# One clamp of the weights' decode goes from VectorE to GpSimd, ahead of VectorE's steps on the low word and the sign

## The chip, the cores and the metric

The kernel runs on one core of a Trainium2 chip. The metric is the device time of one execution in microseconds. Three runs of the kernel before took 1301.26, 1301.65 and 1302.59 us; the median is 1301.65. Engines are named as in the profile: PE is TensorE (PEld its weight loads), DVE VectorE, ACT ScalarE, POOL GpSimd, SP the queue that issues most DMAs.

## The reference

Talking-heads attention (4 batches, 12 heads, 448 positions, 64 per head) feeds two feed-forward layers over 1792 tokens of 768 values:

```
scores = einsum('bhij,hg->bgij', q @ k.T / 8, w_pre);  attn = softmax(scores)
x = (einsum('bhij,hg->bgij', attn, w_post) @ v) as (1792, 768)
a = x @ w1;  b = x @ w2;  h = (a * b) @ w3;  x = h @ w_out          # 768 -> 1024 -> 1024 -> 768
h = x @ w_in;  out = max(h, 0)**2 @ w_out2                          # 768 -> 2048 -> 768
```

All weights arrive as 64-bit floats.

## The kernel before

The chip's engines have no 64-bit floats, so every weight is decoded: from the low word, the high word and the sign bit a 32-bit float is put together by bit operations. The high word's magnitude, clamped, shifted left, gives most of the bits; three bits come from the low word, and the sign from the high word again.

Everything is multiplied with split operands: a float is a high half plus a low half, and a product is three matmuls (high x high, high x low, low x high).

The program has four stages on TensorE. Up to about 500 us it runs attention, then, to 676 us, the products with w1 and w2. From 676 to 749 us stands what the title calls the weights' product: M = w3 x w_out, 1024 x 768, made once on the chip so that the tokens are multiplied with M alone (line 1198, `m_tile`). From 749 us on come the tokens' products with M (line 964, `product`), and then the last layer.

The weights' product is the stage of the change. w3 comes in 16 pieces of 128 x 512, called W1 to W16 here, in the order of `M_ORDER`; each is decoded by `decode_alone`. Its steps are: ACT takes the magnitude of the high word (line 676); DVE takes the three bits of the low word (the shift, 677) and adds the sign (680), into tile `xa`; DVE clamps the magnitude (684), shifts it (687) in tile `zt`, and joins both by an exclusive or (690). Then `one_steps` copies the weight to a high half on ACT (872), and POOL subtracts to get the low half (875). There are 16 copies of these, three buffers for `xa`, one for `zt`, two for the raw weight.

TensorE spends 24 matmuls on each of W1 to W12: four rows of w_out, six matmuls each, over two halves `o` of M's 768 columns. The first two of a row's three kinds of matmul want the high half of the weight, the third its low half. W13 to W16 are used twice, 12 matmuls each time: first for half 0 of the columns, then for half 1. When two pieces of M are ready, `keep_m` copies them from PSUM (ACT, 1181) and DVE takes their largest magnitudes (982, tile `mx`).

When a half of M is complete, `scale_m` finds one scale for it: the largest value is turned by TensorE (1227), reduced on DVE (1230), spread over the partitions by TensorE (1236), and DVE makes the scale (109 to 114, 1242). Then `halves_steps` splits the 8 tiles of that half: high halves on ACT (1129), low halves on DVE (1125). The tokens' products that follow are called c0, c1, c2 (they need half 0 of M) and c3 to c5 (half 1), 24 matmuls each; each is copied from PSUM by ACT (1327), and then DVE reduces it (982, tile `xm`). The next layer's weights are decoded meanwhile (703 to 717).

The order on each engine is written out when the program is built. A stream of steps for the weights (`weight_steps`) stands beside the products; each step names an engine and an assumed cost. `tick` moves an assumed clock on after every few matmuls, and each stream then issues its steps as long as the assumed load of their engine (`busy`) is not too far ahead of that clock; a step marked REST waits for a time on it, and `after(E)` until engine E's assumed load is done. POOL steps cost nothing there. So a changed list of costs or rests changes what stands between what on an engine.

Of the kernel before, what the change touches and what calls it, by code (L numbers as in the profile page):

```python
# [14 lines left out]
ALU = mybir.AluOpType  # L15
# [5 lines left out]
F64_LEAST = 2.0 ** -15 * 1.125  # L21
F64_MOST = float.fromhex("0x1.dffffep+16")
# [13 lines left out]
def talking_heads_attention_moe_moe2(  # L36
# [15 lines left out]
    nc = tc.nc  # L52
# [612 lines left out]
    def after(eng):  # L665
        return REST, Behind(eng), None

    def decode_alone(raw, n):

        lo, hi = (raw.rearrange("p (f two) -> p f two", two=2)[:, :, w] for w in (0, 1))  # L670
        x = pools["w"].tile([P, DM], F32, tag="xa", name="xa", bufs=3)[:, :n]
        zt = pools["w"].tile([P, DM], F32, tag="zt", name="zt", bufs=1)[:, :n]
        xi, zi = x.bitcast(I32), zt.bitcast(I32)
        r = n / DM
        return x, [
            (ACT, 0.9 * r, lambda: nc.scalar.activation(zt, hi.bitcast(F32), AF.Abs)),
            (DVE, 0.55 * r, lambda: nc.vector.tensor_scalar(
                xi, lo, 29, 0x40000000, op0=ALU.logical_shift_right, op1=ALU.bitwise_or
            )),
            (DVE, 0.95 * r, lambda: nc.vector.scalar_tensor_tensor(  # L680
                xi, hi, -(2 ** 31), xi, op0=ALU.bitwise_and, op1=ALU.bitwise_or
            )),
            after(ACT),
            (DVE, 0.55 * r, lambda: nc.vector.tensor_scalar(
                zt, zt, F64_LEAST, F64_MOST, op0=ALU.max, op1=ALU.min
            )),
            (DVE, 0.55 * r, lambda: nc.vector.tensor_scalar(
                zi, zi, 4, 1, op0=ALU.logical_shift_left, op1=ALU.logical_shift_right
            )),
            (DVE, 0.95 * r, lambda: nc.vector.tensor_tensor(xi, zi, xi, op=ALU.bitwise_xor)),  # L690
            after(DVE),
        ]

# [29 lines left out]
    ACT, DVE, POOL, REST, GATE = range(5)  # L723
# [794 lines left out]
```

## Time and profile before

| | us |
|---|---|
| median of three runs | 1301.65 |
| the profiled execution | 1300.97 |
| its span, first to last instruction | 1299.2 |
| PE busy | 1264.7 (97%) |
| DVE busy | 981.1 (76%) |
| ACT busy | 697.0 (54%) |
| POOL busy | 444.5 (34%) |

The granted clock of TensorE is 0.997 of full speed over the span, and 1.00 in the stage of the change. A busy TensorE over the span does not mean that it is busy everywhere: the time of a stage is read from that stage's rows. A duration in the timeline begins when the instruction begins on its engine, and it holds what the instruction itself waited for in hardware; what stands in brackets behind a row is the idle time of the engine just before it, and who ended it.

### The profile page before, as it was taken

What the parts mean: (1) busy time and instruction counts of PE and PEld (TensorE: products, weight loads), DVE (VectorE), ACT (ScalarE), POOL (GpSimd) and SP (SyncE); (2) the same over time, 40 slices, a digit from 0 to 9 for tenths busy, and PEclk for the clock granted to TensorE, in tenths of its full rate; (3) what the DMA queues carried; (4) which work ended last, traced back from release to release, by engine and by line L of the source; (5) the groups of instructions that cost most, each with busy time, mean ns of one, the idle gap of its engine ahead of it and who ended that gap; (6) DMA issues with size and microseconds to landing.
All of it is one profiled execution on the core that took longest, in us unless ns stands there. A gap on an engine that the chain in (4) does not pass through costs nothing.

```text
span 1299.2 us, 25896 instructions
## 1 busy us (share of the span) xinstructions
PE 1264.7 (97%) x10173; PEld 778.9 (60%) x10173; DVE 981.1 (76%) x2036; ACT 697.0 (54%) x1349; POOL 444.5 (34%) x511
## 2 busy tenths in 40 slices
PE   7999999999999899999999999999999999999998
PEld 3676766666766655555569855555555555555555
DVE  5888798788888858877649677336659788797776
ACT  3877876887886535544324354236853453534420
POOL 3899789889877701100002201000000100001000
PEclk9999999999999899999999999999999999999999
DMA  6466555645647624434414332303131322224004
GB/s 176 116 161 158 132 145 135 156 127 149 162 113 196 193 78 94 114 101 99 145 47 138 109 78 56 31 5 86 37 78 45 104 58 60 78 37 109 10 9 170
DMA packets 82174, 132.92 MB, mean 102 GB/s; under 512 B 30820, under 2 KB 67812, under 8 KB 82052
## 3 DMA queue, kind: packets, MB, share of 16 engines
q1 hardware_dynamic: 75636, 121.87, 35.0%
q0 software_dynamic: 2992, 5.42, 2.9%
q10 hardware_dynamic: 3424, 3.98, 1.1%
q8 instruction: 80, 1.31, 0.5%
q14 instruction: 42, 0.34, 0.1%
HBM read 80.78 MB, written 11.92 MB: 71 GB/s over the span
## 4 chain that ended last, share of the span: by engine, by line
PE 86%; DVE 5%; DMA 2%; issue 2%; POOL 2%; ACT 2%; SPq 0%; POOLq 0%; ACTq 0%; DVEq 0%
PE mm L964 40%; PE mm L1395 17%; PE p L272 9%; PE o L365 7%; PE s L232 5%; PE a L476 4%; PE mm L1198 3%; DMA Bt<-S 2%; DVE ATl L387 1%; DVE EL L352 1%; PE p L964 1%; DVE st L286 1%; POOL EH L338 1%; ACT ATh L381 1%; DVE Vl L455 1%
## 5 line engine op out<-in xcount | busy, mean ns | idle before, releaser
L964 PE MATMUL mm<-x,w 128*128 128x448 f16 x2196 | 416.7, 352 | 0.9 <-DVE th L999 0.9
L964 PEld LDWEIGHTS <-w 128*128 128x128 f16 x2304 | 225.0, 98 | 210.4 <-issue 1.3
L1395 PE MATMUL mm<-w,g 128*128 128x384 f16 x1344 | 219.7, 326 | 0.0
L1395 PEld LDWEIGHTS <-g 128*128 128x128 f16 x1344 | 131.5, 98 | 87.4 <-issue 0.2
L272 PE MATMUL p<-Bt,wpre_k 120*120 120x448 f32 x360 | 162.6, 570 | 7.8 <-DMA Bt<-S 3.9
L338 POOL TENSOR_SCALAR EH<-E,st 120x448 f16<-120x448 f32 x180 | 135.7, 764 | 61.6 <-DVE st L324 46.5
L365 PEld LDWEIGHTS <-EH 120*112 120x112 f16 (+1 forms) x1440 | 126.1, 131 | 50.2 <-issue 40.1
L387 DVE TENSOR_TENSOR ATl<-o,ATh 112x480 f16<-112x480 f32 x180 | 116.2, 646 | 39.5 <-ACT ATh L381 39.4
L381 ACT CAST ATh<-o 112x480 f16<-112x480 f32 x180 | 101.1, 562 | 65.2 <-PE o L365 57.5
L365 PE MATMUL o<-wph,EH 120*112 120x120 f16 x720 | 125.7, 220 | 6.1 <-DVE ATl L387 4.5
L294 ACT ACTIVATE E<-p,st 120x448 f32<-120x448 f32 x180 | 116.1, 645 | 22.7 <-DVE st L286 10.2
L729 POOL DMA_DIRECT2D across<-tot x23 | 12.8, 557 | 323.9 <-ACT xa L715 323.9
L365 PE MATMUL o<-wph,EL 120*112 120x120 f16 x720 | 123.5, 217 | 0.0
L365 PE MATMUL o<-wpl,EH 120*112 120x120 f16 x720 | 123.5, 217 | 0.0
L1404 DVE SCALAR_TENSOR_TENSOR acc<-mm,sv,acc 128x384 f32<-128x384 f32 x196 | 112.1, 611 | 14.2 <-PE mm L1395 13.5
L286 DVE TENSOR_REDUCE st<-p 120x1 f32<-120x448 f32 x180 | 110.2, 612 | 7.8 <-PE p L272 7.5
L964 PE MATMUL mm<-h,M 128*128 128x448 f16 x576 | 109.4, 352 | 0.0
L350 POOL TENSOR_TENSOR EL<-F,EH 120x448 f16<-120x448 f32 (+1 forms) x90 | 101.1, 1123 | 7.5
L243 ACT COPY S<-s 110x896 f32<-110x896 f32 (+1 forms) x92 | 84.0, 913 | 27.7 <-PE s L232 27.4
L715 ACT ACTIVATE xa<-xa 128x768 f32<-128x768 f32 x56 | 47.1, 842 | 91.7 <-DVE xa L711 76.3
L365 PEld LDWEIGHTS <-EL 120*112 120x112 f16 x720 | 94.3, 131 | 0.0
L352 DVE SCALAR_TENSOR_TENSOR EL<-E,st,EH 120x448 f16<-120x448 f32 (+1 forms) x90 | 82.5, 917 | 13.3 <-POOL EH L338 12.9
(194 smaller groups left out, 2030.7 us busy)
## 6 DMA issues: line engine op xcount, KB each, us to landing
Bt<-S SPq DMA_DIRECT2D x176, 210.0 KB
raw<-in_moe_w_out_dram SPq DMA_DIRECT2D x24, 768.0 KB
raw<-in_moe_w_in_dram SPq DMA_DIRECT2D x16, 768.0 KB
raw<-in_moe_w_dram SPq DMA_DIRECT2D x14, 768.0 KB
raw<-in_moe_w_dram SPq DMA_DIRECT2D x16, 512.0 KB
vraw<-in_v_dram SPq DMA_DIRECT2D x24, 224.0 KB
out_dram<-acc SPq DMA_DIRECT2D x28, 192.0 KB
kraw<-in_k_dram SPq DMA_DIRECT2D x22, 224.0 KB
```

The costliest lines, as they stand in the source:

```text
L272: nc.tensor.matmul(pt[: n * H, :S], wpre_k.rearrange("p t g -> p (t g)")[: n * H, : n * H], Bt.pop(u)[: n * H], start=True, stop=True,)
L286: nc.vector.tensor_reduce(nsum[u][:n, 0, j : j + 1], Pp[u][:n, :S], axis=AX.X, op=ALU.max, negate=True)
L294: nc.scalar.activation(e[:n], Pp.pop(u)[:n, :S].rearrange("p (a b) -> p a b", a=EG), AF.Exp, bias=t[:n, 0, j : j + 1], scale=1.0, accum_ou ...
L338: nc.gpsimd.tensor_scalar(seven(EH[u][:n]), Ex[u][:n], inverse(u), 1.0, op0=ALU.mult, op1=ALU.mult)
L350: nc.gpsimd.tensor_tensor(a, f, b, op=ALU.subtract)
L352: nc.vector.scalar_tensor_tensor(a, e, inverse(u), b, op0=ALU.mult, op1=ALU.subtract)
L365: nc.tensor.matmul(pt[:CP, c * n : (c + 1) * n], a[:n, c * CP : (c + 1) * CP], w[:n, :n], start=(i == 0), stop=(i == 2),)
L381: nc.scalar.copy(ATs[s][0][:, :, :, m * NR : m * NR + nr], src)
L387: nc.vector.tensor_tensor(ATs[s][1][:, :, :, a], src, ATs[s][0][:, :, :, a], op=ALU.subtract)
L964: nc.tensor.matmul(pt[:, :S], w[a][:, cs], x[z][:, sl], start=(c == 0 and i == 0), stop=(c == len(parts) - 1 and i == 2),)
L1395: nc.tensor.matmul(pt[:, :OH], gs[j][a][:, ts_], ws[j][0][:, w, os_], start=(n == 0), stop=(n == 5),)
L1404: nc.vector.scalar_tensor_tensor(d, pt[:, :OH], sv[:, v : v + 1], d, op0=ALU.mult, op1=ALU.add)
```

## The change

In `decode_alone` the clamp of the magnitude goes from DVE to POOL, and in the order of issue it stands right behind ACT's step. DVE's shift and sign step come after it, then a rest of 0.4 us and the two last steps. The assumed costs of DVE's four steps are higher by 0.05 (times two thirds). The other decode, `decode`, is not touched.

```
             (ACT, 0.9 * r, lambda: nc.scalar.activation(zt, hi.bitcast(F32), AF.Abs)),
-            (DVE, 0.55 * r, lambda: nc.vector.tensor_scalar(
+            after(ACT),
+            (POOL, 0, lambda: nc.gpsimd.tensor_scalar(
+                zt, zt, F64_LEAST, F64_MOST, op0=ALU.max, op1=ALU.min
+            )),
+            (DVE, 0.6 * r, lambda: nc.vector.tensor_scalar(
                 xi, lo, 29, 0x40000000, op0=ALU.logical_shift_right, op1=ALU.bitwise_or
             )),
-            (DVE, 0.95 * r, lambda: nc.vector.scalar_tensor_tensor(
+            (DVE, 1.0 * r, lambda: nc.vector.scalar_tensor_tensor(
                 xi, hi, -(2 ** 31), xi, op0=ALU.bitwise_and, op1=ALU.bitwise_or
             )),
-            after(ACT),
-            (DVE, 0.55 * r, lambda: nc.vector.tensor_scalar(
-                zt, zt, F64_LEAST, F64_MOST, op0=ALU.max, op1=ALU.min
-            )),
-            (DVE, 0.55 * r, lambda: nc.vector.tensor_scalar(
+            (REST, 0.4, None),
+            (DVE, 0.6 * r, lambda: nc.vector.tensor_scalar(
                 zi, zi, 4, 1, op0=ALU.logical_shift_left, op1=ALU.logical_shift_right
             )),
-            (DVE, 0.95 * r, lambda: nc.vector.tensor_tensor(xi, zi, xi, op=ALU.bitwise_xor)),
+            (DVE, 1.0 * r, lambda: nc.vector.tensor_tensor(xi, zi, xi, op=ALU.bitwise_xor)),
```

On POOL nothing else stands among the 16 low halves of this stage, so its order now is clamp, low half, clamp, low half, and so on: each clamp behind the low half of the weight ahead. Behind `decode_alone` every line number is one higher in the changed kernel; in it the clamp is 678, the shift 681, the sign 684, the second shift 688 and the exclusive or 691.

DVE in the weights' product, the decode of W8, one of the weights whose decode lies beside two reductions of finished pieces of M. Before:

```order
L677 TENSOR_SCALAR xa<-raw 128x512
L680 SCALAR_TENSOR_TENSOR xa<-raw,xa 128x512
L982 TENSOR_REDUCE mx<-st 128x1 x2
L684 TENSOR_SCALAR zt<-zt 128x512
L687 TENSOR_SCALAR zt<-zt 128x512
L690 TENSOR_TENSOR xa<-zt,xa 128x512
```

With the change:

```order
L983 TENSOR_REDUCE mx<-st 128x1 x2
L681 TENSOR_SCALAR xa<-raw 128x512
L684 SCALAR_TENSOR_TENSOR xa<-raw,xa 128x512
L688 TENSOR_SCALAR zt<-zt 128x512
L691 TENSOR_TENSOR xa<-zt,xa 128x512
```

The clamp is gone from DVE, and the reductions stand ahead of the shift. It is so at W8 to W11 and W14; at W15 they stood ahead of the shift before as well. The other weights have no reductions beside them.

DVE behind the stage, where the scale of half 1 of M is found while TensorE runs c1 (`most` and `ms` belong to that scale, `xa` and `zt` to a weight of the next layer, `xm` to the reduction of a token product). Before:

```order
L1230 TENSOR_REDUCE most<-mm 1x1
L717 SCALAR_TENSOR_TENSOR xa<-raw,xa 128x768
L704 TENSOR_SCALAR xa<-raw 128x768
L708 TENSOR_SCALAR zt<-zt 128x768
L109 TENSOR_SCALAR ms<-mm 128x1
L110 TENSOR_SCALAR ms<-ms 128x1
L113 TENSOR_SCALAR ms<-ms 128x1
L114 RECIPROCAL ms<-ms 128x1
L1242 TENSOR_SCALAR rows_11170<-rows,ms 128x8
L982 TENSOR_REDUCE xm<-mm 128x1
```

With the change:

```order
L1231 TENSOR_REDUCE most<-mm 1x1
L718 SCALAR_TENSOR_TENSOR xa<-raw,xa 128x768
L705 TENSOR_SCALAR xa<-raw 128x768
L983 TENSOR_REDUCE xm<-mm 128x1
L709 TENSOR_SCALAR zt<-zt 128x768
L712 SCALAR_TENSOR_TENSOR xa<-zt,xa 128x768
L109 TENSOR_SCALAR ms<-mm 128x1
L110 TENSOR_SCALAR ms<-ms 128x1
L113 TENSOR_SCALAR ms<-ms 128x1
L114 RECIPROCAL ms<-ms 128x1
L1243 TENSOR_SCALAR rows_11170<-rows,ms 128x8
```

The reduction of c1 and a joining step of the weight's decode now stand ahead of the scale. On TensorE the turn (1227) goes from c0's end to the middle of c1, and the spread (1236) from the middle of c1 to its end; in half 0 both go 9 matmuls further on.

DVE a little later, the low halves of the 8 tiles of half 1 (numbered `M_11816` to `M_11823` before, `M_11825` to `M_11832` now), about the reduction of c2. Before, the sixth to eighth tile:

```order
L1125 SCALAR_TENSOR_TENSOR M_11820<-st,rows_11170,M_11820 128x384
L1125 SCALAR_TENSOR_TENSOR M_11821<-st,rows_11170,M_11821 128x384
L1125 SCALAR_TENSOR_TENSOR M_11822<-st,rows_11170,M_11822 128x384
L982 TENSOR_REDUCE xm<-mm 128x1
L1125 SCALAR_TENSOR_TENSOR M_11823<-st,rows_11170,M_11823 128x384
```

With the change, the first to fifth tile:

```order
L1126 SCALAR_TENSOR_TENSOR M_11825<-st,rows_11170,M_11825 128x384
L1126 SCALAR_TENSOR_TENSOR M_11826<-st,rows_11170,M_11826 128x384
L1126 SCALAR_TENSOR_TENSOR M_11827<-st,rows_11170,M_11827 128x384
L983 TENSOR_REDUCE xm<-mm 128x1
L1126 SCALAR_TENSOR_TENSOR M_11828<-st,rows_11170,M_11828 128x384
L1126 SCALAR_TENSOR_TENSOR M_11829<-st,rows_11170,M_11829 128x384
```

The reduction of c2 stood behind seven low halves, and stands behind three. On ACT a step of the weight's decode (715) stands behind the second high half of these tiles, and the copy of c2 from PSUM (1327) behind the fifth. The order of the SP queue is the same.

## Rows read from the trace of the kernel before

**Rows 1.** Busy time by stretch; columns: PE, PEld, DVE, ACT, POOL, clock, DMA.

```profile
750.00:800.00 50.00, 50.00 (x266) 25.87 (x265) 32.42 (x69) 22.84 (x41) 4.08 (x6) 1.00 0.36 75
```

**Rows 2.** Groups, 640 to 760 us: busy us, mean ns; idle before, and releasers.

```profile
L1198 PE MATMUL mm<-late,w 128*128 128x384 f32 x192 | 35.4, 340 | 3.4 <-POOL w L875 2.1 <-ACT w L872 1.3
L1198 PE MATMUL mm<-wo,w 128*128 128x384 f32 x192 | 34.5, 338 | 0.5 <-POOL w L875 0.5
```

**Rows 3.** Timeline of PE: start us, us, engine, line, operation; W11 and W12, then W16.

```profile
719.33 8.48 PE L1198 MATMUL mm<-late,w 128*128 128x384 f32 x48
...
738.52 2.00 PE L1198 MATMUL mm<-late,w 128*128 128x384 f32 x10 [0.73 <-POOL w L875]
```

**Rows 4.** Timeline, from W6's copy to W7's copy.

```profile
696.47 0.62 ACT L872 CAST w<-xa 128x512 fp32r<-128x512 f32 x1 [2.48 <-DVE xa L690]
...
697.00 0.67 ACT L676 ACTIVATE zt<-raw 128x512 f32<-128x512 f32 x1
697.17 1.41 POOL L875 TENSOR_TENSOR w<-xa,w 128x512 fp32r<-128x512 f32 x1 [2.28 <-ACT w L872]
697.70 1.17 DVE L684 TENSOR_SCALAR zt<-zt 128x512 f32<-128x512 f32 x1 [0.28 <-ACT zt L676]
...
698.90 0.43 DVE L687 TENSOR_SCALAR zt<-zt 128x512 int32<-128x512 int32 x1
699.36 0.69 DVE L690 TENSOR_TENSOR xa<-zt,xa 128x512 int32<-128x512 int32 x1
...
700.14 0.62 ACT L872 CAST w<-xa 128x512 fp32r<-128x512 f32 x1 [0.73 <-DVE xa L690]
```

**Rows 5.** Timeline: W5's clamp and copy, W14's low half, W15's sign, W16's copy and low half.

```profile
691.07 0.42 DVE L684 TENSOR_SCALAR zt<-zt 128x512 f32<-128x512 f32 x1
...
692.79 0.62 ACT L872 CAST w<-xa 128x512 fp32r<-128x512 f32 x1 [3.99 <-DVE xa L690]
...
729.13 1.55 POOL L875 TENSOR_TENSOR w<-xa,w 128x512 fp32r<-128x512 f32 x1 [2.87 <-ACT w L872]
729.57 1.66 DVE L680 SCALAR_TENSOR_TENSOR xa<-raw,xa 128x512 int32<-128x512 int32 x1
...
736.50 0.62 ACT L872 CAST w<-xa 128x512 fp32r<-128x512 f32 x1 [2.47 <-DVE xa L690]
...
737.20 1.27 POOL L875 TENSOR_TENSOR w<-xa,w 128x512 fp32r<-128x512 f32 x1 [2.26 <-ACT w L872]
```

**Rows 6.** One line of the attention: ns of one, least, median and most.

```profile
L349 POOL TENSOR_SCALAR F<-E,st x90: 637/1002/1887, 29.6 to 450.4; 120x448 f32<-120x448 f32 x88, 96x448 f32<-96x448 f32 x2
```

**Rows 7.** Timeline behind the stage: scales, copies and c0 to c2.

```profile
746.26 4.16 ACT L1129 ACTIVATE M<-st,rows 128x384 f16<-128x384 f32 x8 [4.63 <-DVE rows L1242]
...
749.36 4.71 PE L964 MATMUL mm<-h,M 128*128 128x448 f16 x24
...
754.17 0.63 ACT L1327 ACTIVATE st<-mm,ms 128x448 f32<-128x448 f32 x1 [0.68 <-PE mm L964]
...
755.16 0.84 ACT L715 ACTIVATE xa<-xa 128x768 f32<-128x768 f32 x1 [0.36 <-DVE xa L711]
...
756.69 43.49 PE L964 MATMUL mm<-h,M 128*128 128x448 f16 x229
...
757.95 0.15 DVE L109 TENSOR_SCALAR ms<-mm 128x1 f32<-128x1 f32 x1
...
758.97 1.12 ACT L1129 ACTIVATE M<-st,rows 128x384 f16<-128x384 f32 x2 [2.07 <-DVE rows L1242]
```

**Rows 8.** Groups of DVE, 750 to 770 us.

```profile
L1125 DVE SCALAR_TENSOR_TENSOR M<-st,rows,M 128x384 f16<-128x384 f32 x11 | 6.1, 613 | 0.0
L982 DVE TENSOR_REDUCE xm<-mm 128x1 f32<-128x448 f32 x4 | 2.5, 616 | 1.7 <-ACT st L1327 1.7
...
L711 DVE SCALAR_TENSOR_TENSOR xa<-zt,xa 128x768 int32<-128x768 int32 x2 | 1.9, 956 | 0.0
...
L708 DVE TENSOR_SCALAR zt<-zt 128x768 f32<-128x768 f32 x3 | 1.7, 550 | 0.5 <-ACT zt L703 0.5
```

## The prediction

> **What bounds the kernel now.** I read the page first (PE busy 97% of the span), then the busy time by stretch, the groups of the stretch around the changed lines, and the order of time there. After 750 us TensorE does not pause: the row of 750 to 800 us has 50.00 of 50 us busy [rows 1]. So whatever TensorE loses or gains before that point goes into the total one for one. The reader is to see that the stage of the changed function (TensorE's L1198, 676 to 749 us) is one where TensorE does wait: 0.5 and 3.4 us, and every one of these waits is for POOL's L875 or ACT's L872, the last two steps of a decoded weight [rows 2]. I call the 16 pieces of the first weight W1 to W16. TensorE spends 24 matmuls on each of W5 to W12, that is 8.48/2 = 4.24 us a piece; the last four are used half as long, and there it outruns the decoder: before W16's low half, for one, it stands still until L875 is done and starts again at 738.52 [rows 3]. So the stage ends when W16's L875 ends, and that is the end of a chain of decodes that runs from W5's copy (692.79) to W16's copy (736.50) without being far ahead anywhere: 43.71 us for 11 steps [rows 5].
>
> **What one step costs now.** From one copy L872 to the next, W6 to W7: L875 starts 0.70 after the copy and takes 1.41; DVE's clamp L684 ends 0.29 later, and the shift L687 starts 0.03 after that; 0.46 to the xor L690, 0.78 to the next copy. 0.70 + 1.41 + 0.32 + 0.46 + 0.78 = 3.67 [rows 4]. The row to look at is L684: it started at 697.70, while L875 ran, and took 1.17 us, where alone it takes 0.42 (W5's) [rows 4, 5]. It did not run slowly: it waited until L875 was through and then needed 0.29. L680, the step on the sign, shows the same: 1.66 us beside an L875 that had 1.55, and it ends 0.55 after it [rows 5]. So each of these DVE steps and a GpSimd instruction exclude each other, and the time on that shared path, not DVE's work as such, is what fills the step.
>
> The Trainium skill has a rule for this ("SBUF — State Buffer", "Who interferes with whom"): a DVE step that streams one tensor through both ports, or one that reads two tensors from SBUF, and a GpSimd instruction that reads SBUF block each other wholly, for the whole instruction. The two rows above agree; no row shows the clamp itself on GpSimd beside these steps. By the rule, the shift on the low word and the sign step do not stand beside the new clamp but before or behind it, and the total is the sum below; without it, it is the first rival's.
>
> **The change part by part.** *Removed:* the clamp on DVE, 16 times, worth 0.32 us in a plain step. *Added:* the clamp on GpSimd. The nearest row is L349, GpSimd's float32 instruction with one input of 448 columns: 0.64 us when nothing is in its way, 1.0 at the median, 1.9 at most [rows 6]. 512 columns give 0.64 x 512/448 = 0.73 at most, as some of it does not grow with columns. I take 0.72; the bounds are 0.64, and 1.0, that median. Below nothing it cannot go. (The Trainium skill, "GPSIMD Engine Reference", "Elementwise — side-by-side cycle accounting", gives 769 ns for 512 elements of a one-input loop; 0.05 more per step would be 0.5 us in the sum.)
>
> *Where it stands:* GpSimd works in order, and the clamp of a weight is issued behind L875 of the weight ahead. So it is not free to start when ACT's magnitude is ready (0.53 + 0.67 after the copy) but only when L875 is done, 0.9 us later. A plain step is then 0.70 + 1.41 + 0.72 + 0.03 + 0.46 + 0.78 = 4.10, which is 0.43 more than now.
>
> *Moved:* the two reductions L982, which six times stood between the sign step and the clamp (where DVE waited for L875 anyway) or ahead of the shift, now all six times stand ahead of the shift. The shift then meets L875, and the sign step meets the clamp. Such a step is 0.70 to L875, 1.27 for it (W16's, with nothing in its way), 0.29 for the rest of the shift, 0.59 for the clamp (0.72 less the 0.13 that a held-up instruction has done before, as 0.42 less 0.29), 0.55 for the sign step, 0.38 until the xor (its 0.46, started 0.08 early), 0.78: 4.56 [rows 4, 5]. A step of this kind stands in the trace already: W14 to W15, with the clamp still on DVE, took 4.42.
>
> Of the 11 steps, 5 are plain and 6 have the reductions: 5 x 4.10 + 6 x 4.56 = 47.86, against 43.71: +4.15. Before W5 DVE runs the four L855 on two SBUF tensors, and the clamp has to get between them: 0.72 in place of 0.42, rounded to +0.2 with what is hidden (bounds 0 and 0.3). TensorE's own pace (4.24) is no longer slower than the decoder, so it waits a little at W9 to W11 as well; all of that is inside the sum, because the stage still ends on W16's L875. **First term: +4.35.**
>
> *Orders further on.* The steps' costs for the planner change, and so does what stands behind the stage. At its end the second half of the product's scale is found (L1227, L1236, L109 to L1242), and 8 tiles are split into halves for TensorE's third product (c3). In the changed order DVE has the reduction of the second product (c1) and L708 and L711 of a weight ahead of L109, and ACT has L715 between the second and third copy and the eviction of c2 ahead of the sixth; DVE's reduction of c2 stands between the third and the fourth low half. Count from the start T of c0 (749.36 now). c1 ends at 756.69 + 12 x 0.196 = T + 9.7, as 24 matmuls take 4.71. Its eviction starts 0.1 later and takes 0.63: T + 10.4; reduction 0.62, L708 0.55, L711 0.96: T + 12.5; from L109 to the first copy 758.97 - 757.95 = 1.02: T + 13.6. Copies go every 0.52, L715 takes 0.84: five copies and L715 are through at T + 17.0, the eviction of c2 at 17.7, its reduction at 18.3, the fourth low half (0.61) at 18.9. TensorE begins c3 at T + 14.4 and wants that half 11 matmuls on, at T + 16.6 [rows 7, 8]. It comes 2.3 late. What follows comes every 0.6, about as fast as TensorE asks (3 x 0.196). Now TensorE has no pause there [rows 1]. Bounds: 0, if one of these steps gets ahead, and 2.6, with 0.03 for each of ten hand-overs. **Second term: +2.3.** The first half's chain is later by 9 matmuls, 1.6 us, against a cover of over 2 us that the present row of L1129 shows (first copy at 746.26, c0 at 749.36): nothing.
>
> *At nothing:* the changed costs on the shift, sign and xor steps only move when they are issued; the DMA queue issues the same transfers in the same order, each behind the sign step of the weight two before it, which covers it with a whole step. W1 to W4 are decoded before the stage or at its start, ahead of their use; without that cover each would cost the 0.43 of a plain step.
>
> Sum: 4.35 + 2.3 = 6.65 on the profiled execution's 1300.97: 1307.6. The median of the runs shown, 1301.65, is 0.7 above that execution, within the spread of the runs, and I leave it at 1307.6.
>
> **Rivals.** *The clamp does run beside DVE's steps.* For: no row shows a one-input GpSimd instruction against exactly these steps. Against: L349, which has one input, is spread from 0.64 to 1.9 us. Then all 11 steps are 4.10, 45.1 in all, +1.4; W5 comes 0.45 earlier as its clamp is off DVE; with the second term 1.4 - 0.5 + 2.3 = +3.2: 1304.2.
>
> *The other side: no slower.* The same, and DVE, which has 16 clamps of 0.42 to 1.17 us less, reaches the third product's halves early enough that c3 does not wait. It decides if the fourth low half is ready 11 matmuls into c3. For it: DVE's queue is shorter. Against it: the halves wait for TensorE's c1 and c2, not for DVE's work. Price +0.9: 1301.9. If besides that W14 to W16 came in time, TensorE's 3.9 us of waits would go, and the kernel would be faster, 1298; GpSimd's queue speaks against it, as L875 and clamp alone are 2.1 us between two copies.
>
> *A dearer clamp.* If GpSimd is held up at the clamp as L349 was at its median, 1.0: 11 x 0.28 = 3.1 more: 1310.7.
>
> **How the numbers follow.** Forecast 0.67 (own range 1304.5 to 1309.5, clamp 0.64 and no wait in c3 at the lower end), dearer clamp 0.12, clamp beside DVE 0.09, no slower 0.09, faster 0.03. A measurement here tells about 0.2%, 2.6 us, from no change: above 1304.25 is slower. Faster 0.03; within 0.2%: 0.09 and a share of the two cases whose ends come near the bound, 0.13 in all; slower 0.84. The range is 1303.3 to 1311.
>
> **What would show it.** Right: L872 to L872 of W6 to W7 at about 4.1 and of W8 to W9 at about 4.6; the clamp on GpSimd starting when L875 ends; the shift on the low word at well over 1 us in the steps with reductions; TensorE's waits in the stage at 8 us and over where they were 3.9; a wait of about 2 us of TensorE in the third product for a low half. Wrong: the sign step at 0.69 while the clamp runs (then there is no exclusion), a clamp far from 0.7, or TensorE running through c3.

## The result and the profile after

The changed kernel takes 1322.98 us (median of five runs, 1321.74 to 1323.74); the kernel before, run on the same chip, 1302.43 (1301.26 to 1305.68). The ratio is 1.0148, with an interval of 1.0138 to 1.0159: some 20 us slower. The forecast was 1307.6, the range ended at 1311. The direction was right, and the size was three times too small.

The clamp on GpSimd, and TensorE's waits in the stage, 640 to 790 us (groups: busy us, mean ns; idle before, and who ended it):

```profile
L678 POOL TENSOR_SCALAR zt<-zt 128x512 f32<-128x512 f32 x16 | 33.0, 2065 | 52.1 <-ACT zt L676 52.1
...
L1199 PE MATMUL mm<-late,w 128*128 128x384 f32 x192 | 39.5, 354 | 8.7 <-POOL w L876 4.5 <-ACT w L873 4.2
...
L1199 PE MATMUL mm<-wo,w 128*128 128x384 f32 x192 | 37.5, 351 | 4.7 <-ACT w L873 2.4 <-POOL w L876 2.3
```

The clamp takes 2.07 us on average where the prediction put 0.72. TensorE waits 13.4 us for the decoder where it waited 3.9 [rows 2].

One plain step, from W6's copy to W7's (start us, us), which answers to [rows 4]:

```profile
701.87 0.62 ACT L873 CAST w<-xa 128x512 fp32r<-128x512 f32 x1 [4.08 <-DVE xa L691]
...
702.57 1.39 POOL L876 TENSOR_TENSOR w<-xa,w 128x512 fp32r<-128x512 f32 x1 [2.01 <-ACT w L873]
...
703.93 1.92 POOL L678 TENSOR_SCALAR zt<-zt 128x512 f32<-128x512 f32 x1
...
705.88 0.43 DVE L688 TENSOR_SCALAR zt<-zt 128x512 int32<-128x512 int32 x1 [3.06 <-POOL zt L678]
706.35 0.69 DVE L691 TENSOR_TENSOR xa<-zt,xa 128x512 int32<-128x512 int32 x1
...
707.13 0.62 ACT L873 CAST w<-xa 128x512 fp32r<-128x512 f32 x1 [3.32 <-DVE xa L691]
```

The chain is the predicted one, link by link: copy, low half, clamp as soon as the low half is done, second shift, exclusive or, copy. DVE does nothing for 3.06 us before line 688, so nothing on DVE holds the clamp up, and yet it takes 1.92 us. The step is 5.26 us where it was 3.67.

A step with reductions, W7 to W8 (DVE, then POOL), answering to [rows 5]:

```profile
707.88 1.51 DVE L681 TENSOR_SCALAR xa<-raw 128x512 int32<-128x512 int32 x1
...
709.43 0.98 DVE L684 SCALAR_TENSOR_TENSOR xa<-raw,xa 128x512 int32<-128x512 int32 x1
711.20 0.43 DVE L688 TENSOR_SCALAR zt<-zt 128x512 int32<-128x512 int32 x1 [0.80 <-POOL zt L678]
```

```profile
707.83 1.28 POOL L876 TENSOR_TENSOR w<-xa,w 128x512 fp32r<-128x512 f32 x1 [1.98 <-ACT w L873]
709.08 2.08 POOL L678 TENSOR_SCALAR zt<-zt 128x512 f32<-128x512 f32 x1
```

The shift waits for the low half, as predicted: it ends 0.28 after it. The sign step does not wait for the clamp: it starts and ends inside it, with 0.98 us for the 0.69 it takes alone, and the clamp takes 0.16 more. So steps with reductions are no longer than plain ones, about 5.3 us both.

Not every DVE step is free of the clamp. W4's shift, which starts with the clamp, takes its 0.42 us. W5's starts 1.53 us into its clamp, takes 0.85 and ends 0.28 behind it, as it would behind a low half (W4, then W5):

```profile
684.59 2.28 POOL L678 TENSOR_SCALAR zt<-zt 128x512 f32<-128x512 f32 x1 [20.98 <-ACT zt L676]
684.68 0.42 DVE L681 TENSOR_SCALAR xa<-raw 128x512 int32<-128x512 int32 x1
...
692.32 2.10 POOL L678 TENSOR_SCALAR zt<-zt 128x512 f32<-128x512 f32 x1 [2.23 <-ACT zt L676]
693.85 0.85 DVE L681 TENSOR_SCALAR xa<-raw 128x512 int32<-128x512 int32 x1
```

From W5's copy to W16's, and from TensorE's pace at the end of the stage, the rest can be read off (ACT; PE; then busy time by window, with the columns of [rows 1], where the granted clock stands behind POOL):

```profile
696.59 0.62 ACT L873 CAST w<-xa 128x512 fp32r<-128x512 f32 x1 [4.36 <-DVE xa L691]
...
754.84 0.62 ACT L873 CAST w<-xa 128x512 fp32r<-128x512 f32 x1 [4.08 <-DVE xa L691]
```

```profile
678.82 1.38 PE L1199 MATMUL mm<-wo,w 128*128 128x384 f32 x6
...
751.74 2.01 PE L1199 MATMUL mm<-late,w 128*128 128x384 f32 x10 [0.88 <-POOL w L876]
756.87 3.29 PE L1199 MATMUL mm<-late,w 128*128 128x384 f32 x10 [0.73 <-POOL w L876]
...
769.00 6.98 PE L965 MATMUL mm<-h,M 128*128 128x448 f16 x36
...
784.66 1.40 PE L965 MATMUL mm<-h,M 128*128 128x448 f16 x5 [0.21 <-ACT M L1130]
787.38 2.82 PE L965 MATMUL mm<-h,M 128*128 128x448 f16 x14 [1.32 <-DVE M L1126]
```

```profile
751.00:756.00 5.00, 2.50 (x12) 1.99 (x12) 1.25 (x3) 1.00 (x2) 3.03 (x3) 1.00 0.50 165
756.00:762.00 6.00, 5.26 (x23) 5.13 (x23) 1.31 (x4) 0.48 (x1) 0.81 (x1) 0.72 0.01 3
```

Eleven steps take 754.84 - 696.59 = 58.25 us, against 43.71. Between the stage's first matmul and W5's copy it is 17.77 against 16.68 (the clamps of W4 and W5 lie there). After W16's copy ten matmuls take 3.29 us where the same ten took 2.00 [rows 3]: behind 5 us in which TensorE was busy for 2.50, the granted clock is 0.72 over the next 6 us, part of them at the lower level of 1.2 GHz. And TensorE stands still for M in c3, as foreseen: from c0's start to the end it is 1321.0 - 769.00 = 552.0, against 1299.2 - 749.36 = 549.84.

In sum: +14.54 in the steps, +1.09 ahead of them, +1.30 of clock behind them, so 90.18 us from the stage's first matmul to c0 where it was 73.25, and +2.16 after c0: 19.1 us. The two profiled spans differ by 21.8; the other 2.7 lie ahead of the stage, where nothing is changed yet (the first clamp on GpSimd comes at 643.00). At 600 us TensorE already has 419 matmuls left before the stage where it had 405, and at 0.19 us each those 14 are the 2.7 (before, then changed):

```profile
599.66 76.78 PE L964 MATMUL mm<-x,w 128*128 128x448 f16 x405
```

```profile
599.72 79.42 PE L965 MATMUL mm<-x,w 128*128 128x448 f16 x419
```

### The profile page after: what moved, and what is told of

Same layout as the page of the kernel before. It is cut to its first block, busy times and chain, and to the rows that moved or that the text cites. A ratio compares the mean times of both kernels' runs of the same rounds, so it can differ in the third digit from the quotient of the medians.

```text
span 1321.0 us, 25882 instructions
## 1 busy us (share of the span) xinstructions
PE 1273.3 (96%) x10173; PEld 780.6 (59%) x10173; DVE 981.6 (74%) x2020; ACT 695.7 (53%) x1349; POOL 473.0 (36%) x527
## 3 DMA queue, kind: packets, MB, share of 16 engines
q10 hardware_dynamic: 3424, 3.98, 1.2%
## 4 chain that ended last, share of the span: by engine, by line
PE 65%; DVE 13%; issue 6%; POOL 5%; DMA 5%; ACT 5%; SPq 0%; ACTq 0%; POOLq 0%; DVEq 0%
PE mm L965 24%; PE mm L1396 17%; PE p L272 8%; PE o L365 7%; PE s L232 4%; PE a L476 4%; DMA Bt<-S 3%; POOL zt L678 2%; DMA ac<-across 1%; DVE xa L712 1%; POOL EH L338 1%; DVE h L1126 1%; DVE ATl L387 1%; ACT xa L716 1%; DVE xa L691 1%
```

## The experiments

Two theories stood after the result. *The form:* this instruction, a maximum and then a minimum by two constants, is dear on GpSimd wherever it stands. The row that the price was taken from, L349, is a product and another product. *The neighbours:* GpSimd is held up in this place, by DVE or by ACT, as L349 was at its median, or the changed order costs the time. Three lengths separate the terms in each trace: W5's copy to W16's (the steps), the stage's first matmul to c0 (the whole stage), and c0 to the end (the third product's wait). All of it is in this table, worked out from each profile as above, in us:

| kernel | clamp in a plain step | W5 to W16 | stage | c0 to end |
|---|---|---|---|---|
| before | 1.17 (0.42 alone), DVE | 43.71 | 73.25 | 549.84 |
| changed | 1.92 | 58.25 | 90.18 | 552.00 |
| two products on GpSimd | 0.61 | 46.58 | 75.94 | 552.04 |
| maximum alone | 1.49 | 53.53 | 83.32 | 552.07 |
| changed, clamp on DVE | 1.17 (0.42 alone), DVE | 46.10 | 75.67 | 552.05 |
| before, clamp on GpSimd | 1.92 | 58.05 | 88.70 | 549.87 |
| low halves on DVE | 0.42, DVE | 42.29 | 72.51 | 552.03 |
| the same, planned at 0 | 0.42, DVE | 42.17 | 71.24 | 549.92 |

**The instruction by itself.** Behind the end of the kernel before, GpSimd runs forms of it on spare tiles, first alone, then some of them beside one DVE instruction; the kernel's time says nothing here. `MX`, `MN` and `MU` are maximum, minimum and product; the two calls with one operation are lines 1464 and 1465.

```
...
+    def ts(o, x, c0, c1, f0, f1, n=512):
+        nc.gpsimd.tensor_scalar(o[:, :n], x[:, :n], c0, c1, op0=f0, op1=f1)
+    for n in (512, 256):
+        ts(p0, s0, 1.0, 1.0, MU, MU, n)
+        ts(p0, s0, F64_LEAST, F64_MOST, MX, MN, n)
+        nc.gpsimd.tensor_scalar(p0[:, :n], s0[:, :n], F64_LEAST, None, op0=MX)
+        nc.gpsimd.tensor_scalar(p0[:, :n], s0[:, :n], 1.0, None, op0=MU)
+    ts(p0, p0, F64_LEAST, F64_MOST, MX, MN)
+    ts(p0, p0, 1.0, 1.0, MU, MU)
+    ts(p0, s0, 1.0, F64_MOST, MU, MN)
+    ts(p0, s0, 1.0, 1.0, MU, ALU.add)
...
```

> The kernel before, with GpSimd instructions on spare tiles behind its end, first alone (no VectorE work), then in pairs with a VectorE step that starts 0.6 us later. Its time tells nothing. Theory A (the form of the clamp is dear): max with min on 128x512 takes 1.9 us alone, the product with two constants about 0.72, and at 256 columns both fall to about half plus a fixed part. Theory B (the clamp was held up by VectorE in the changed kernel): max with min alone takes about 0.72, as the products do. For the pairs: if the two engines exclude each other for whole instructions, a VectorE shift and a VectorE sign step both end only after GpSimd's instruction (1.5 us and more beside a 1.9 us clamp); if only GpSimd's reads are in the way, the sign step beside the clamp stays near 0.69 while the shift waits.

Measured alone, in order of time: two products; maximum only; product only; maximum and minimum; product and minimum; product and sum:

```profile
1299.78 0.61 POOL L1459 TENSOR_SCALAR bn<-bn 128x512 f32<-128x512 f32 x1 [51.20 <-DVE bn L1455]
...
1302.48 1.49 POOL L1464 TENSOR_SCALAR bn<-bn 128x512 f32<-128x512 f32 x1
1304.06 1.49 POOL L1465 TENSOR_SCALAR bn<-bn 128x512 f32<-128x512 f32 x1
...
1309.14 1.92 POOL L1459 TENSOR_SCALAR bn<-bn 128x512 f32<-128x512 f32 x1
...
1311.84 1.92 POOL L1459 TENSOR_SCALAR bn<-bn 128x512 f32<-128x512 f32 x1
1313.85 0.62 POOL L1459 TENSOR_SCALAR bn<-bn 128x512 f32<-128x512 f32 x1
```

With no neighbour at all the clamp takes 1.92 us, as in the stage, and two products 0.61. The form decides, and one operation alone is dearer than two products. The Trainium skill ("GPSIMD Engine Reference", "Elementwise — side-by-side cycle accounting") gives, as the best case of a loop, 769 ns measured for 512 elements. The six rows lie on both sides of that, from 0.61 to 1.92 us.

Beside a DVE instruction that starts half a microsecond later (clamp and shift, clamp and sign, subtraction and shift, subtraction and sign; POOL, then DVE):

```profile
1315.20 1.92 POOL L1459 TENSOR_SCALAR bn<-bn 128x512 f32<-128x512 f32 x1 [0.73 <-ACT bn L1473]
1317.85 1.91 POOL L1459 TENSOR_SCALAR bn<-bn 128x512 f32<-128x512 f32 x1 [0.73 <-ACT bn L1473]
...
1323.22 1.26 POOL L1483 TENSOR_TENSOR bn<-bn,bn 128x512 f32<-128x512 f32 x1 [0.76 <-ACT bn L1473]
1325.21 1.26 POOL L1483 TENSOR_TENSOR bn<-bn,bn 128x512 f32<-128x512 f32 x1 [0.73 <-ACT bn L1473]
```

```profile
1315.67 0.43 DVE L1486 TENSOR_SCALAR bn<-bn 128x512 int32<-128x512 int32 x1 [13.93 <-ACT bn L1475]
...
1318.32 0.69 DVE L1489 SCALAR_TENSOR_TENSOR bn<-bn 128x512 int32<-128x512 int32 x1 [1.01 <-ACT bn L1475]
...
1323.69 1.08 DVE L1486 TENSOR_SCALAR bn<-bn 128x512 int32<-128x512 int32 x1 [0.62 <-ACT bn L1475]
...
1325.68 1.33 DVE L1489 SCALAR_TENSOR_TENSOR bn<-bn 128x512 int32<-128x512 int32 x1 [0.86 <-ACT bn L1475]
```

The two-tensor subtraction keeps DVE out until it is through (the shift ends 0.29 behind it, the sign step 0.54). The clamp does not: 0.43 and 0.69 are the times alone. The rule of the Trainium skill in the prediction ("SBUF — State Buffer", "Who interferes with whom") holds here for the subtraction, and on these tiles not for the clamp. W5's shift above did wait for a clamp; it started 1.53 us into it, these two steps 0.47 us into it. Whether that is the reason was not tried.

**The same place, a cheap form.** In the changed kernel two products by 1.0 stand for the clamp; the clamping is left out.

```
-                zt, zt, F64_LEAST, F64_MOST, op0=ALU.max, op1=ALU.min
+                zt, zt, 1.0, 1.0, op0=ALU.mult, op1=ALU.mult
```

> The changed kernel, with GpSimd's max and min replaced by two products with 1.0 (the bounds of the clamp are left out). Same orders on all engines. Theory A (the form of the clamp is dear): GpSimd's step takes about 0.72 in place of 1.92, the steps from copy to copy 4.1 and 4.6 us in place of 5.3, the stage falls by 11 x 1.2 less what the other steps hide, about 9 to 12 us, and the total is about 1309 us (6.6 above the kernel before, as the prediction's sum has it). Theory B (VectorE holds the instruction up): it stays at 1.9 and the total near 1323.

1308.15 us, ratio 1.0046 (1.0032 to 1.0060). The chain behind W6's copy, on POOL:

```profile
699.58 1.40 POOL L876 TENSOR_TENSOR w<-xa,w 128x512 fp32r<-128x512 f32 x1 [2.00 <-ACT w L873]
...
700.95 0.61 POOL L678 TENSOR_SCALAR zt<-zt 128x512 f32<-128x512 f32 x1
```

Plain steps are 3.98 us, those with reductions 4.45. Everything but the form is the changed kernel's, and over two thirds of the loss are gone (0.46% in place of 1.48%). The neighbours are not the cause.

**A price in between.** The lower bound alone.

```
-                zt, zt, F64_LEAST, F64_MOST, op0=ALU.max, op1=ALU.min
+                zt, zt, F64_LEAST, None, op0=ALU.max
```

> The changed kernel with the lower bound alone on GpSimd (one operation, max); the upper bound is left out. Measured by itself at the end of a run of the kernel before, this form took 1.49 us on 128x512 (max and min together 1.92, two products 0.62). Theory (the step is the clamp's time plus a constant 3.36 us, since 0.62 gave steps of 3.98 and 1.92 gave 5.28): steps of 4.85 us, 53.4 us from the fifth piece's copy to the sixteenth's where the changed kernel has 58.25, so about 5 to 6 us less than the changed kernel: 1317 us. Rival (max is as dear as the clamp when VectorE works beside it, or the step is held by something other than the clamp): steps stay at 5.28 us and the time at 1322 to 1324 us.

1316.56 us, ratio 1.0096 (1.0080 to 1.0112). Two copies, W6's and W7's:

```profile
700.89 0.62 ACT L873 CAST w<-xa 128x512 fp32r<-128x512 f32 x1 [3.65 <-DVE xa L691]
...
705.72 0.62 ACT L873 CAST w<-xa 128x512 fp32r<-128x512 f32 x1 [2.89 <-DVE xa L691]
```

Steps of 4.83 to 4.90 against 4.85 expected. A plain step is 3.36 us and the clamp, at three prices: in a plain step the clamp's own time counts one for one.

**The order without the engine.** The changed list, costs and rest; the clamp on DVE, behind the sign step.

```
-            (POOL, 0, lambda: nc.gpsimd.tensor_scalar(
-                zt, zt, F64_LEAST, F64_MOST, op0=ALU.max, op1=ALU.min
-            )),
...
+            (POOL, 0, lambda: nc.vector.tensor_scalar(
+                zt, zt, F64_LEAST, F64_MOST, op0=ALU.max, op1=ALU.min
+            )),
```

> The changed kernel's list of costs, rests and steps and its orders, with the clamp issued on VectorE at its old place behind the sign step: the change without its engine. Theory A (the clamp's form on GpSimd is the cost, the orders add the wait in the third product): steps without reductions 3.67 as before, steps with reductions 4.4, TensorE waits about 2.2 us in the third product; 3 to 4 us above the kernel before, about 1306. Rival C (the new orders cost most of it): 1315 and more. If the orders cost nothing: 1302.5.

1307.19 us, ratio 1.0033 (1.0020 to 1.0046). The order alone costs 4.6 us by the table: 2.39 in the steps, because the reductions ahead of the shift put the shift beside the low half (1.53 us at W8), and 2.21 behind c0. Steps with reductions are 4.62 us, where 4.4 was expected. So with the cheap form nearly all of the loss is the order's.

**The engine without the order.** The kernel before, and only the clamp's engine changed.

```
-            (DVE, 0.55 * r, lambda: nc.vector.tensor_scalar(
+            (DVE, 0.55 * r, lambda: nc.gpsimd.tensor_scalar(
                 zt, zt, F64_LEAST, F64_MOST, op0=ALU.max, op1=ALU.min
```

> The kernel before with its list and all its orders, only the clamp's engine changed: GpSimd clamps, VectorE's shift and sign step and the reductions stand where they stood. Theory A: every step from copy to copy is 0.70 + 1.41 + 1.92 + 0.03 + 0.46 + 0.78 = 5.3 us, 11 x 5.3 = 58.3 against 43.7, no wait in the third product; with half a us at W5 and some us where the granted clock falls, 15 to 18 us above the kernel before, 1317 to 1321. Rival C (the orders cost it): about 1305, and steps of about 4.

1320.65 us, ratio 1.0134 (1.0121 to 1.0147). Its c0, and the rest of c1 with c2 and c3, on PE:

```profile
770.03 4.71 PE L964 MATMUL mm<-h,M 128*128 128x448 f16 x24
...
777.37 22.87 PE L964 MATMUL mm<-h,M 128*128 128x448 f16 x120
```

The step is as long as the changed kernel's, and the wait in c3 is not there (120 matmuls without a pause): the clamp's price and the order's are separate, and the third product's wait belongs to the order. Since the step is now longer than any order of DVE's work, the order's 2.4 us in the steps do not come on top.

**What the step would gain from GpSimd's absence.** If the low half's subtraction keeps DVE's clamp waiting, the gain lies in taking that off GpSimd. In the kernel before, DVE subtracts, behind the next weight's sign step.

```
+    pend = []
+    def held():
+        return [(DVE, 0.6, pend.pop())] if pend else []
...
+            *held(),
             after(ACT),
...
-            nc.gpsimd.tensor_tensor(ll, x, hh, op=ALU.subtract)
+            (nc.vector if kind == "w3" else nc.gpsimd).tensor_tensor(
+                ll, x, hh, op=ALU.subtract
+            )
...
-        yield POOL, 2.0, low
+        if kind == "w3" and chunks[i + 1][0] == "w3":
+            pend.append(low)
+            return
+        yield (DVE, 0.6, low) if kind == "w3" else (POOL, 2.0, low)
```

> The kernel before with the low half's subtraction of the sixteen pieces on VectorE, issued behind the next piece's sign step (where a piece of another kind follows, at once). Theory (in the kernel before a step of 3.68 us is copy, then GpSimd's subtraction of 1.4 us, and VectorE's clamp ends only behind that): without a GpSimd instruction in the step it is VectorE's five steps and the subtraction, some 3.2 us plain and 4.2 with reductions; 39 to 41 us from the fifth copy to the sixteenth where the kernel before has 43.71. TensorE has 71.4 us of matmuls in 73.25 us from the stage's first to the first token product, so at most 1.9 us can be saved: 1300.5 to 1302.5 us in a session where the kernel before has 1302.5. Rival (VectorE becomes the bound, or the third product waits longer for M because a reduction is issued later): steps over 3.9 us or a wait of 1 to 3 us before a token product, 1303 to 1306 us.

1304.46 us, ratio 1.0001 (0.9992 to 1.0010). The theory was right on the steps (3.18 and 4.11) and the rival on the time: the stage is 0.74 shorter and the part behind c0 2.19 longer. The turn for the first scale, c0, the spread of the second scale and c3, on PE:

```profile
746.34 0.27 PE L1238 MATMUL mm<-ident,most 128*1 128x128 f32 x1
...
750.77 1.58 PE L975 MATMUL mm<-h,M 128*128 128x448 f16 x6 [1.02 <-ACT M L1140]
...
762.03 0.38 PE L1247 MATMUL mm<-most,ones 1*128 1x1 f32 x2 [0.49 <-DVE most L1241]
...
768.62 11.71 PE L975 MATMUL mm<-h,M 128*128 128x448 f16 x61 [1.18 <-DVE M L1136]
```

The planner saw more load on DVE and put that turn later. c0 waits for M, which is why the stage gains only 0.74, and behind c0 TensorE waits for the second scale and for a low half of M.

**The same with a planned cost of 0**, so that no other instruction moves at the end of the stage.

```
-        return [(DVE, 0.6, pend.pop())] if pend else []
+        return [(DVE, 0, pend.pop())] if pend else []
...
-        yield (DVE, 0.6, low) if kind == "w3" else (POOL, 2.0, low)
+        yield (DVE, 0, low) if kind == "w3" else (POOL, 2.0, low)
```

> As the kernel with the low halves on VectorE, but with a planned cost of 0 for each, so that every other instruction stands in the order of the kernel before, the third product's preparation too. Theory (the 2.2 us that the former gave back came from the order, in which the first maximum's transposition stood 10 matmuls later): 549.8 us from the first token product to the end as in the kernel before, where the former had 552.0, and 72.3 to 73.0 us from the stage's first matmul to that product where the kernel before has 73.25; in all 0.3 to 1.5 us less than the kernel before, ratio 0.9988 to 0.9998. Rival (the 2.2 us come from VectorE's added load itself, or the stage is held by TensorE and nothing is left to gain): 551 to 552 us from the first token product, or 73.2 us before it; ratio 1.000 to 1.001.

1300.93 us, ratio 0.9983 (0.9974 to 0.9992): faster than both kernels. A plain step on DVE, and the turn and c0 on PE:

```profile
696.13 0.68 DVE L881 TENSOR_TENSOR w<-xa,w 128x512 fp32r<-128x512 f32 x1
696.73 0.42 DVE L690 TENSOR_SCALAR zt<-zt 128x512 f32<-128x512 f32 x1
697.19 0.43 DVE L693 TENSOR_SCALAR zt<-zt 128x512 int32<-128x512 int32 x1
```

```profile
742.77 0.27 PE L1238 MATMUL mm<-ident,most 128*1 128x128 f32 x1
...
749.68 4.71 PE L975 MATMUL mm<-h,M 128*128 128x448 f16 x24
```

DVE's clamp takes 0.42, not 1.17 [rows 4], although DVE now does more. The stage is 71.24 us, 2.0 less than before, where 0.3 to 0.9 was expected: 1.54 less in the steps and 0.61 less behind W16's copy, where DVE makes the last low half in 0.69 us and POOL took 1.27 [rows 5], against 0.14 more ahead of W5's copy. The 71.4 us of matmuls that the expectation before this one took for a floor were too many. The part behind c0 is the old 549.9: the 2.2 us came from the order, and not from DVE's load.

## Why the prediction was wrong

**The step that failed** is the price of the clamp: "I take 0.72; the bounds are 0.64, and 1.0, that median." It takes 1.92. The row under it, L349, was read by its shape (one input, float32, 448 columns) and not by its operations: it multiplies twice. Two products on 512 columns do take 0.61, so the scaling by columns was sound, and applied to another instruction. The spread of L349 to 1.89 was seen, and put down to hold-ups only. For a plain step the prediction's own sum with 1.92 in it is 0.70 + 1.41 + 1.92 + 0.03 + 0.46 + 0.78 = 5.30, against 5.26 measured. The rival of a dearer clamp had the direction, but bounded it by that same row.

**The exclusion** was right for the low half, and for the sign step beside the clamp it was wrong. The steps with reductions were put 0.46 longer than plain ones, since the sign step was to stand behind the clamp. With 1.92 that sum gives 5.76 for each of six steps, some 0.46 too much, 2.8 us in all; what was measured is 0.29 of delay, which does not reach the end of the step. So with the price put right the prediction's eleven steps come to 5 x 5.30 + 6 x 5.76 = 61.06, and less the 2.8 to 58.3, where 58.25 was measured. With the cheap form these steps measured 4.45, and the same sum gives 4.56 - 0.11; there the two readings cannot be told apart, because the clamp is short. With the maximum alone they can: W8's sign step takes the same 0.98, inside a GpSimd step of 1.66.

**The second term** was right: +2.3 forecast, +2.16 measured, in the place named, and it stays with the changed order in all four kernels that have it. That c0 would not wait was right too.

**The rest.** Ahead of W5's copy +0.2 was forecast and 1.09 came. Of that, 0.72 is there at W4's copy (9.27 us behind the stage's first matmul, 8.55 before), whose decode was put at nothing as covered; W5's steps on DVE stand behind L856, which waits for ACT's L853 behind W4's copy. The 1.30 us of lower clock behind W16's copy was not foreseen, and was not tried by itself. The kernel before with only the engine changed had a granted clock of 0.50 from 751 to 756 us, and yet 12.87 us from W16's copy to c0, as the kernel before (12.86) and not 14.16 as the changed kernel: there the lower clock fell where TensorE waited for the decoder in any case. With the clamp at its predicted price, the two-product kernel, the sum comes near: 6.65 forecast, 2.69 + 2.20 = 4.9 by the table, and 6.0 by the ratio (4.2 to 7.8).

What stays open is why a maximum, or one operation alone, is so much dearer on GpSimd than two arithmetic ones, and what decides when a DVE step waits beside the clamp: why the sign step loses 0.29 us in the stage and nothing on the spare tiles, and W5's shift 0.43. In the stage the raw words that DVE reads lie two apart, on the spare tiles side by side; that was not tried by itself.

## What to carry to other kernels

Take a price for an instruction on another engine from a row with the same operations, not only the same shape; where there is none, measure it behind the end of a kernel before moving it. Where an engine's instruction is long because it waits for another engine's, try moving the one that blocks: here that gained 2.2 us, and moving the one that was blocked cost 20. And where a planner orders the work, a changed cost is a change of its own: give a new instruction the cost that keeps the order, and the two effects can be seen apart.

## What the runs showed of the hardware

- GpSimd, one input of 128x512 float32: product and product 0.61 us, product and sum 0.62, maximum or product alone 1.49, maximum and minimum 1.92, product and minimum 1.92.
- A GpSimd subtraction of two tensors (1.26 us) keeps a DVE shift and a DVE sign step out to its end; the clamp on GpSimd (1.92 us) let both run at their own speed on spare tiles. In the stage the sign step took 0.98 us beside it in place of 0.69, and a shift that started 1.53 us into a clamp ended 0.28 behind it.
- In the changed kernel, where TensorE waited for the decoder, its granted clock was 0.66 from 746 to 751 us and 0.72 from 756 to 762, in a stage where it had been 1.00; ten matmuls took 3.29 us in place of 2.00.
